# Attention and SoLU on one core: aligned arrays, centring on ScalarE, clamps on GpSimd, and a new list of steps

## The chip, the core and the metric

The kernel runs on one core of a Trainium2 chip. The metric is the device time of one execution in microseconds. The engines are named as in the profile: PE is TensorE, PEld its weight loads, DVE is VectorE, ACT is ScalarE, POOL is GpSimd, SP the engine that issues most DMAs. Each engine takes its own instructions strictly in the order of its list and waits at an instruction whose inputs or buffers aren't ready.

## The reference

Windowed attention (8 batches, 8 heads, 576 positions, 64 wide), then a SoLU block over all 4608 tokens. Half of the heads attend to the last 32 positions, half to every fourth of the last 128.

```python
scores = scale * np.matmul(q, k.transpose(0, 1, 3, 2))
scores = np.where(masks[None, :, :, :], scores, -1000000000.0)
attn = softmax(scores) @ v                      # per head
x = attn.transpose(0, 2, 1, 3).reshape(B * S, H * D)   # 4608 x 512
h = x @ w_in                                    # 4608 x 1024
e = np.exp(h - h_max)
solu = h * e / (np.sum(e, axis=-1, keepdims=True) + 1e-09)
mu = np.mean(solu, axis=-1, keepdims=True)
var = np.mean((solu - mu) ** 2, axis=-1, keepdims=True)
ln = (solu - mu) / np.sqrt(var + 1e-06) * g_ln
out = ln @ w_out                                # 4608 x 512
```

The softmax is abridged here. The weights w_in and w_out arrive as 64-bit floats, whose words the kernel turns into 32-bit floats itself.

## The kernel before, in words

**Units and tiles.** Attention is cut into 32 units (two heads of one batch each), taken one at a time for units 0 to 3 (steps S, max, sub, exp, sum, inv, norm, turn, V, x) and two at a time from there (the same names with a p in front, pS2 for units 4 and 5). The tokens are 36 tiles of 128, in 18 pairs; four units, one batch, give the 576 tokens of four and a half tiles.

**Weights.** Each of 16 blocks of 128x512 64-bit words (0 to 7 of w_in, 8 to 15 of w_out) is loaded (w) and converted: abs and low on ACT pick the upper and lower words, clamp (L261) bounds the magnitude, sign (L267) and join (L274) on DVE put the bits together, gain multiplies w_out's rows by g. Every float is then split into a high and a low half (hi, lo), since products run with 32-bit operands rounded for PE and each product takes three matmuls: high by high, high by low, low by high. The low half is either a difference on PE copied by ACT (diff and lo, LOW_DIFF "m") or a subtraction on POOL ("p").

**Products.** Tiles 0 to 3, the first two pairs, are computed plainly: ha, hb, hc, hd are quarters of x @ w_in (6 matmuls of 512 columns each; 24 a tile). All later pairs use seven products Ma to Mg of sums instead of eight. For these, eight sums of weight blocks are made once (ta to td, each for j = 0 and 1, L316), with their own high and low halves (ua to ud on ACT, va to vd by the subtraction of L296), and sums of x for every pair (s on DVE, hS and lS its halves).

**SoLU.** For a tile: peak (the maximum, L533, where h is in PSUM), e (the exponential, L537), gate (L543: h times e, its sum in mu), mid (L551 scales mu, L557 subtracts the mean), var (a square on ACT, L562, and six one-column instructions on POOL), t (8 transposes on PE, L577), th and tl (halves of the transposed tile, L584 and L296), o (24 matmuls with w_o, L606), out (L613 scales by 1/sigma, and a DMA).

**Buffers.** Everything has a fixed address in SBUF. t and e are two buffers each, th and tl two each, ob one; qt, kt and vt are four each, so that unit 4's v is loaded into unit 0's buffer. The conversions borrow them: mag (the magnitudes) lies in slots of the weight sums and in ob, low in x_sum and in slot w12, and the 64-bit words in t, e, th and tl. All arrays begin at multiples of 64 bytes; the identity matrices, the mask and minus begin 128 above a multiple of 512, w_i, w_o, x, t, e, sm, pt, qt, kt and vt 384 above one, and the slots w8 to w13, th and tl 192 above.

**Order.** No scheduler moves anything. ORDER is one long list of steps, written out in the source; the program walks it once, and each step appends its instructions to the lists of its engines. A step early in ORDER thus stands early on every engine that it uses, including the two DMA queues. The loads of one SP list follow each other too: one that waits for its buffer holds up those behind it.

Of the kernel before, what the change touches and what calls it, by code (L numbers as in the profile page):

```python
# [38 lines left out]
POOL_NORM = ()  # L39
ACT_MID = ()  # L40
# [3 lines left out]
LOW_DIFF = "mmmmmmpppppppppp"  # L44
# [74 lines left out]
def windowed_attention_then_solu_kernel(  # L119
# [26 lines left out]

    id_sb = fixed("id_sb", [P])
    minus = fixed("minus", [P], F32R)
    id_bf = fixed("id_bf", [2 * P], BF16)[:, 0:P]
    mask_sb = fixed("mask_sb", [2, NS * WQ], BF16)  # L150
# [14 lines left out]
    g_sb = fixed("g_sb", [FT])  # L165
    mx_sb = fixed("mx", [2, 2, NS])
    rs_sb = fixed("rs", [2, 2, NS])
    pk_sb = fixed("pk", [2, 2])
    mhalf = fixed("mhalf", [1])
    below = fixed("below", [1])  # L170
# [89 lines left out]
    def conv_clamp(b):  # L260
        nc.vector.tensor_scalar(  # L261
            out=mag(b), in0=mag(b), scalar1=F64_MIN, scalar2=F64_MAX, op0=ALU.max, op1=ALU.min
        )
# [43 lines left out]
    def w_sum(k, j):  # L307
        b11, b12, b21, b22 = (mag(b) for b in (2 * j, 2 * j + 1, 4 + 2 * j, 5 + 2 * j))
        out, a, b = {
            "a": (b11, b12, b11),  # L310
            "b": (x_spare[:, 512 * j : 512 * j + 512], b22, b12),
            "c": (b22, b22, b11),
            "d": (b21, b21, b22),
        }[k]
        sums[k, j] = out
        nc.gpsimd.tensor_tensor(out=out, in0=a, in1=b, op=ALU.subtract)  # L316
# [7 lines left out]
    def w_sum_lo(k, j):  # L324
        w = w_sum_slot(k, j)
        rest(nc.gpsimd, w[:, 1, :], sums[k, j], w[:, 0, :])
# [328 lines left out]
    for name in PRODUCTS:  # L655
        do[name] = quick(name)
# [80 lines left out]
```

## Time and profile before

| | |
|---|---|
| median of 3 runs | 562.0 us (561.88 to 562.92) |
| the profiled execution's own time | 561.86 us |
| its span, first to last instruction | 560.1 us |
| mean granted TensorE clock | 0.963 |
| instructions | 16524 |

The page gives the busy time of each engine over the span and then the same in 40 slices of 14 us, in tenths:

```profile
PE   1747678999989999998999999989999999999997
...
DVE  4997999686886668775879767876896966648350
ACT  5658567454634446452554453533644545335350
POOL 0103797844324134150425242331524433021130
PEclk9958959999999999997999999998999999999999
```

In the first seven slices the weights are converted and the first attention units run; behind them PE is the busiest engine. PEclk is the granted TensorE clock, in tenths. A row such as "L606 PE MATMUL banks<-w_o,th" names the line of the program, the engine, the operation, what is written and what is read. In the chain of waits a row is a start, a duration and the engine and line whose end released the next row.

### The profile page before, as it was taken

The page shows a single profiled execution, that of the slowest core. Times are in us where ns is not written, and L with a number is a line of the kernel's source. Part 1 is how long each engine was busy: PE and PEld are TensorE (multiplying, and loading weights), DVE is VectorE, ACT ScalarE, POOL GpSimd, SP SyncE. Part 2 cuts the span into 40 slices and gives each one's busy share as a digit, 9 for nine tenths or more (in the row PEclk, how much of TensorE's full clock was granted, in tenths as well). Part 3 has the DMA queues.
Part 4 walks back from the last instruction along what each step waited for, and adds up shares of the span by engine and source line. Part 5 has one row for each costly group of instructions (what it writes and reads, how often), then busy time and mean ns, then how long its engine had stood idle before and what let it go on. Part 6 is the DMA issues. An engine that isn't in the chain of part 4 may idle for free.

```text
span 560.1 us, 16524 instructions
## 1 busy us (share of the span) xinstructions
PE 504.6 (90%) x7322; PEld 407.3 (73%) x7322; DVE 411.2 (73%) x692; ACT 273.0 (49%) x430; POOL 192.0 (34%) x274
## 2 busy tenths in 40 slices
PE   1747678999989999998999999989999999999997
PEld 0445566787878788886888788777777788888875
DVE  4997999686886668775879767876896966648350
ACT  5658567454634446452554453533644545335350
POOL 0103797844324134150425242331524433021130
PEclk9958959999999999997999999998999999999999
DMA  8967240315113323003052111533222000000001
GB/s 274 372 236 249 93 149 2 94 48 188 73 55 103 98 72 110 22 19 122 20 184 76 64 52 64 167 110 104 73 86 78 20 21 19 20 19 36 23 34 42
DMA packets 22247, 51.66 MB, mean 92 GB/s; under 512 B 2720, under 2 KB 3360, under 8 KB 22176
## 3 DMA queue, kind: packets, MB, share of 16 engines
q1 hardware_dynamic: 22032, 50.48, 26.9%
q8 instruction: 57, 0.93, 0.7%
q10 hardware_dynamic: 144, 0.13, 0.1%
q14 instruction: 14, 0.11, 0.1%
HBM read 41.16 MB, written 9.44 MB: 90 GB/s over the span
## 4 chain that ended last, share of the span: by engine, by line
PE 80%; DVE 9%; DMA 5%; issue 3%; ACT 1%; SPq 1%; ACTq 0%; DVEq 0%
PE banks L606 34%; PE banks L480 29%; PE banks L433 6%; PE banks L577 6%; PE banks L348 5%; DMA vt<-vw 2%; DVE t L557 2%; DMA kt<-kT 1%; DMA t<-w_in 1%; DVE x_sum L267 1%; DVE sm L374 1%; DVE t L543 1%; DVE mx L387 1%; DVE nmax L533 1%; ACT x_raw L449 1%
## 5 line engine op out<-in xcount | busy, mean ns | idle before, releaser
L606 PE MATMUL banks<-w_o,th 128*128 128x512 f32 x576 | 183.0, 401 | 1.2 <-issue 0.8
L606 PEld LDWEIGHTS banks<-w_o,th 128*128 128x128 f32 x576 | 107.5, 189 | 27.1 <-ACT ob L613 1.0
L606 PE MATMUL banks<-w_o,tl 128*128 128x512 f32 x288 | 113.2, 397 | 0.1
L480 PE MATMUL banks<-w_i,x_hi 128*128 128x512 f32 x320 | 104.8, 408 | 1.3 <-issue 1.3
L391 POOL TENSOR_TENSOR sm<-sm,mx 128x1280 f32<-128x1280 f32 x14 | 39.7, 2839 | 131.2 <-DVE mx L387 92.6
L480 PEld LDWEIGHTS banks<-w_i,x_hi 128*128 128x128 f32 x320 | 59.6, 193 | 14.1 <-issue 1.7
L480 PE MATMUL banks<-w_i,x_lo 128*128 128x512 f32 x160 | 64.0, 400 | 2.0 <-DVE sm L374 1.2
L606 PEld LDWEIGHTS banks<-w_o,tl 128*128 128x128 f32 x288 | 54.5, 189 | 14.5 <-issue 1.5
L480 PE MATMUL banks<-w,x_hi 128*128 128x512 f32 x192 | 61.6, 402 | 0.0
L537 ACT ACTIVATE e<-t,nmax 128x1024 f32<-128x1024 f32 x32 | 36.7, 1148 | 49.9 <-DVE nmax L520 49.9
L514 DVE CUSTOM_DVE_ANT_0 t<-banks,t 128x512 f32<-128x512 f32 x64 | 43.3, 686 | 22.8 <-PE banks L480 21.8
L613 ACT ACTIVATE ob<-banks,rstd 128x512 f32<-128x512 f32 x36 | 24.9, 693 | 65.6 <-PE banks L606 46.7
L433 PE MATMUL banks<-pt,vt 32*64 32x64 f32 (+3 forms) x2816 | 37.1, 242 | 20.9 <-issue 8.1
L507 DVE TENSOR_TENSOR t<-banks,t 128x512 f32<-128x512 f32 x32 | 22.1, 690 | 45.7 <-PE banks L480 28.3
L433 PEld LDWEIGHTS banks<-pt,vt 32*64 32x64 f32 x2816 | 34.7, 144 | 27.1 <-issue 11.4
L296 DVE TENSOR_TENSOR tl<-banks,th 128x512 fp32r<-128x512 f32 x72 | 45.9, 678 | 11.3 <-ACT th L584 11.2
L584 ACT CAST th<-banks 128x512 fp32r<-128x512 f32 x72 | 38.9, 594 | 21.2 <-PE banks L606 11.4
L412 POOL TENSOR_TENSOR sm<-sm,rs 128x1280 f32<-128x1280 f32 x14 | 34.0, 2429 | 37.6 <-DVE rs L407 31.9
L562 ACT ACTIVATE e<-t 128x1024 f32<-128x1024 f32 x36 | 38.1, 1059 | 17.6 <-DVE t L557 17.5
L543 DVE CUSTOM_DVE_ANT_0 t<-t,e 128x1024 f32<-128x1024 f32 x32 | 38.9, 1219 | 8.3 <-ACT e L537 8.3
L348 PE MATMUL banks<-kt,qt 64*32 64x64 f32 x2560 | 33.3, 235 | 12.2 <-issue 8.8
L348 PEld LDWEIGHTS banks<-kt,qt 64*32 64x32 f32 x2560 | 28.9, 110 | 20.1 <-issue 14.9
(94 smaller groups left out, 780.3 us busy)
## 6 DMA issues: line engine op xcount, KB each, us to landing
vt<-vw SPq DMA_DIRECT2D x32, 384.0 KB, 4.8
kt<-kT SPq DMA_DIRECT2D x32, 312.0 KB, 4.1
qt<-qT SPq DMA_DIRECT2D x32, 296.0 KB, 4.6
out<-ob SPq DMA_DIRECT2D x35, 256.0 KB, 2.0
e<-w_in SPq DMA_DIRECT2D x2, 512.0 KB, 5.5
t<-w_in SPq DMA_DIRECT2D x2, 512.0 KB, 7.4
t<-w_out SPq DMA_DIRECT2D x2, 512.0 KB, 6.8
e<-w_out SPq DMA_DIRECT2D x2, 512.0 KB, 6.4
```

The costliest lines, as they stand in the source:

```text
L296: eng.tensor_tensor(out=out, in0=whole, in1=part.bitcast(F32), op=ALU.subtract)
L348: nc.tensor.matmul(out=ps[WIN * c : WIN * c + WIN, h, WQ * i : WQ * i + WQ], lhsT=qt[D * h : D * h + D, q0 : q0 + WIN], rhs=kt[D * h : D * ...
L391: eng.tensor_tensor(out=rows(part(sm_sb, us)), in0=soft_source(us), in1=wide(part(mx_sb, us)), op=ALU.subtract,)
L412: eng.tensor_tensor(out=sm, in0=sm, in1=wide(part(rs_sb, us)), op=ALU.mult)
L433: nc.tensor.matmul(out=ps[D * h : D * h + D, c, c0 : c0 + k1 - k0], lhsT=vt[WIN * c : WIN * c + WIN, i, D * h : D * h + D], rhs=pt[WIN * c ...
L480: nc.tensor.matmul(out=ps, lhsT=x[:, xs + k], rhs=weights(ws[k])[:, part, :], start=start and k == 0 and j == 0, stop=stop and k == 1 and ...
L514: nc.vector.tensor_tensor_reduce(out=split_t(k)[half], in0=banks[:, c, :], in1=add, scale=1.0, scalar=-3.0e38, op0=ALU.add, op1=ALU.max, a ...
L537: nc.scalar.activation(out=e_sb[i % 2], in_=h_of(i), func=AF.Exp, bias=ms[i]["nmax"], scale=1.0, accum_out=se)
L543: nc.vector.tensor_tensor_reduce(out=t_sb[i % 2], in0=h_of(i), in1=e_sb[i % 2], scale=1.0, scalar=0.0, op0=ALU.mult, op1=ALU.add, accum_ou ...
L562: nc.scalar.activation(out=e_sb[i % 2], in_=t_sb[i % 2], func=AF.Square, accum_out=sq)
L584: nc.scalar.copy(out=turned("th", i)[:, 4 * c : 4 * c + 4], in_=ps_t(i, c))
L606: nc.tensor.matmul(out=ps_o(i), lhsT=a[:, f, :], rhs=w_o[:, f, part, :], start=k == 0, stop=k == 3 * FT - 1,)
```

## The change

Six things differ.

1. The small arrays (g, the attention's maxima and sums, pk and two constants) become parts of one array, `little`, of 384 bytes, and the mask is padded, so that id, minus, mask, w_i, w_o, all parts of x, t, e, ob, sm, pt, qt, kt, vt, the slots w8 to w13, th and tl begin at multiples of 512 bytes.
2. The centring of every tile (mid) runs on ACT as an activation with a bias; DVE only scales mu by −1/1024 for it.
3. The 16 clamps run on POOL.
4. The eight sums of weight blocks and their eight low halves run on DVE, not POOL; the norms of units 0 to 3 run on POOL, not DVE.
5. Blocks 6 and 7 get their low halves by a difference on PE and a copy on ACT.
6. ORDER is a new list, and in it an output product o (24 matmuls) is four steps oa, ob, oc, od of six, with other steps allowed in between.

```diff
-LOW_DIFF = "mmmmmmpppppppppp"
+LOW_DIFF = "mmmmmmmmpppppppp"
...
+    little = fixed("little", [96])
+    g_sb, mhalf, below = little[:, 0:FT], little[:, 8:9], little[:, 9:10]
+    mx_sb = little[:, 16:36].rearrange("p (u h s) -> p u h s", u=2, h=2)
...
-    mask_sb = fixed("mask_sb", [2, NS * WQ], BF16)
+    mask_sb = fixed("mask_sb", [768], BF16)[:, 0 : 2 * NS * WQ]
...
     def conv_clamp(b):
-        nc.vector.tensor_scalar(
+        nc.gpsimd.tensor_scalar(
             out=mag(b), in0=mag(b), scalar1=F64_MIN, scalar2=F64_MAX, op0=ALU.max, op1=ALU.min
         )
...
         sums[k, j] = out
-        nc.gpsimd.tensor_tensor(out=out, in0=a, in1=b, op=ALU.subtract)
+        nc.vector.tensor_tensor(out=out, in0=a, in1=b, op=ALU.subtract)
...
-        rest(nc.gpsimd, w[:, 1, :], sums[k, j], w[:, 0, :])
+        rest(nc.vector, w[:, 1, :], sums[k, j], w[:, 0, :])
...
-        eng = nc.gpsimd if len(us) == 2 or us[0] in POOL_NORM else nc.vector
-        eng.tensor_tensor(out=sm, in0=sm, in1=wide(part(rs_sb, us)), op=ALU.mult)
+        nc.gpsimd.tensor_tensor(out=sm, in0=sm, in1=wide(part(rs_sb, us)), op=ALU.mult)
...
     def moe_centre(i):
...
+        nc.vector.tensor_scalar(out=mu, in0=mu, scalar1=-1.0 / DF, scalar2=None, op0=ALU.mult)
+        nc.scalar.activation(out=t, in_=t, func=AF.Identity, bias=mu, scale=1.0)
...
-    def moe_o(i, lo=0, hi=3 * FT):
+    def moe_o(i, lo, hi):
...
+    for k, name in enumerate(("oa", "ob", "oc", "od")):
+        do[name] = lambda i, k=k: moe_o(i, 6 * k, 6 * k + 6)
```

What stands beside the steps named here in the two lists, ORDER around pturn3, the transpose of units 6 and 7's probabilities (pV3 is their product with v, t, o and the M products are as above):

```
before: ... peak2 gain15 th0 tl0 hb3 var1 pturn3 hd3 peak3 e2 hi15 q9 gate2 gain14 hi14 pV3 ud0 lo14 e3 gate3
        lo15 mid3 px3 hA2 lo13 o0 ud1 mid2 hB2 lA2 Ma2 vd0 v8 vd1 pS4 ...
after:  ... pnorm3 lo14 hb3 mid2 var2 ua0 tl1 peak3 pturn3 e3 oa0 td0 ob0 oc0 pV3 tc1 va1 td1 ub0 vb0 ud0 od0
        va0 ud1 vd1 vd0 px3 hA2 q8 pS4 ...
```

On PE around pV3, the product of the attention's units 6 and 7 (L433, with vt_93 and vt_94), before (L480 is the last quarter of a plain tile, L606 the first output product):

```order
L480 MATMUL banks<-w_i,x_lo 128x512
L433 MATMUL banks<-pt,vt_93 64x64 x24
L433 MATMUL banks<-pt,vt_93 64x48 x8
L433 MATMUL banks<-pt,vt_93 64x16 x8
L433 MATMUL banks<-pt,vt_94 64x64 x24
L433 MATMUL banks<-pt,vt_94 64x48 x8
L433 MATMUL banks<-pt,vt_94 64x16 x8
L606 MATMUL banks<-w_o,th_1109 128x512 x2
L606 MATMUL banks<-w_o,tl_1112 128x512
```

And at the same place in the changed kernel (L603 is L606 of before, L436 is L433, and vt_94 and vt_95 are units 6 and 7):

```order
L603 MATMUL banks<-w_o,th_1084 128x512 x2
L603 MATMUL banks<-w_o,tl_1087 128x512
L436 MATMUL banks<-pt,vt_94 64x64 x24
L436 MATMUL banks<-pt,vt_94 64x48 x8
L436 MATMUL banks<-pt,vt_94 64x16 x8
L436 MATMUL banks<-pt,vt_95 64x64 x24
L436 MATMUL banks<-pt,vt_95 64x48 x8
L436 MATMUL banks<-pt,vt_95 64x16 x8
L603 MATMUL banks<-w_o,th_1084 128x512 x2
```

Eighteen of the first output product's matmuls now stand ahead of pV3, and six behind it.

On DVE around the first gate and the transpose of units 4 and 5 (pturn2, the STREAM_TRANSPOSE), before; t_76, e_78 and mu belong to tile 0:

```order
L543 ISA t_76,mu<-banks,e_78 128x1024
L543 ISA mu 128x1
L551 TENSOR_SCALAR mu<-mu 128x1
L557 TENSOR_SCALAR t_76<-t_76,mu 128x1024
L261 TENSOR_SCALAR w_290<-w_290 128x512
L267 SCALAR_TENSOR_TENSOR w_107<-tl_756,w_107 128x512
L415 STREAM_TRANSPOSE pt<-sm 128x1280
```

In the changed kernel (t_77 and e_79 are tile 0's there, L546 is L543, L553 is L551, L418 is L415):

```order
L546 ISA t_77,mu<-banks,e_79 128x1024
L546 ISA mu 128x1
L536 TENSOR_REDUCE nmax<-banks 128x1
L553 TENSOR_SCALAR mu<-mu 128x1
L271 SCALAR_TENSOR_TENSOR w_122<-e_80,w_122 128x512
L418 STREAM_TRANSPOSE pt<-sm 128x1280
```

The centring and the clamp are gone from DVE, and tile 1's peak (L536) stands between the gate and mu's scaling. POOL's list begins, behind its constants, with the clamps and the single units' norms:

```order
L265 TENSOR_SCALAR w_100<-w_100 128x512
L265 TENSOR_SCALAR w_111<-w_111 128x512
L265 TENSOR_SCALAR w_100<-w_100 128x512
L265 TENSOR_SCALAR w_111<-w_111 128x512
L415 TENSOR_TENSOR sm<-sm,little 128x640 x2
L265 TENSOR_SCALAR w_243<-w_243 128x512
L265 TENSOR_SCALAR w_303<-w_303 128x512 x2
```

Before, its first array instructions were two sums of weights (L316); all clamps (L265 here) and these norms (L415 here) were DVE's.

More of the change, by code (lines that the diff above doesn't have):

```diff
@@ L38 @@
 PE_MASK = (0, 1, 2, 3)
-POOL_NORM = ()
-ACT_MID = ()
 REBIAS = 2.0**16
@@ L145, in fixed @@
         return const.tile([P, *shape], dtype, name=name)
+    little = fixed("little", [96])
+    g_sb, mhalf, below = little[:, 0:FT], little[:, 8:9], little[:, 9:10]
+    mx_sb = little[:, 16:36].rearrange("p (u h s) -> p u h s", u=2, h=2)
+    rs_sb = little[:, 40:60].rearrange("p (u h s) -> p u h s", u=2, h=2)
+    pk_sb = little[:, 64:68].rearrange("p (k c) -> p k c", k=2)
     id_sb = fixed("id_sb", [P])
@@ L149, in windowed_attention_then_solu_kernel @@
     id_bf = fixed("id_bf", [2 * P], BF16)[:, 0:P]
-    mask_sb = fixed("mask_sb", [2, NS * WQ], BF16)
+    mask_sb = fixed("mask_sb", [768], BF16)[:, 0 : 2 * NS * WQ]
+    mask_sb = mask_sb.rearrange("p (d w) -> p d w", d=2)
     w_i = fixed("w_i", [8, 2, 512], F32R)
@@ L164, in windowed_attention_then_solu_kernel @@
     vts = [fixed(f"vt{k}", [NV, 2 * D]) for k in range(4)]
[L165 to L170, printed above, removed]
     banks = psum.tile([P, 8, 512], F32, name="banks")
@@ L549, in moe_centre @@
         t, mu = t_sb[i % 2], ms[i]["mu"]
-        on_act = i in ACT_MID
-        nc.vector.tensor_scalar(
-            out=mu, in0=mu, scalar1=(-1.0 if on_act else 1.0) / DF, scalar2=None, op0=ALU.mult
-        )
-        if on_act:
-            nc.scalar.activation(out=t, in_=t, func=AF.Identity, bias=mu, scale=1.0)
-        else:
-            nc.vector.tensor_scalar(out=t, in0=t, scalar1=mu, scalar2=None, op0=ALU.subtract)
+        nc.vector.tensor_scalar(out=mu, in0=mu, scalar1=-1.0 / DF, scalar2=None, op0=ALU.mult)
+        nc.scalar.activation(out=t, in_=t, func=AF.Identity, bias=mu, scale=1.0)
     def moe_var(i):
@@ L651, in windowed_attention_then_solu_kernel @@
         "peak": moe_peak, "e": moe_exp, "gate": moe_gate, "mid": moe_centre, "var": moe_var,
-        "t": moe_t, "th": moe_th, "tl": moe_tl, "o": moe_o, "out": moe_out,
-        "oa": lambda i: moe_o(i, 0, 21), "oz": lambda i: moe_o(i, 21),
-    }
+        "t": moe_t, "th": moe_th, "tl": moe_tl, "out": moe_out,
+    }
+    for k, name in enumerate(("oa", "ob", "oc", "od")):
+        do[name] = lambda i, k=k: moe_o(i, 6 * k, 6 * k + 6)
     for name in PRODUCTS:
```

126 rows, old and new, of the table ORDER are left out of this document.

## The prediction

> **What bounds the kernel now.** I begin with the page's busy shares, its PE slices (14 us each) and its chain that ended last, and then read the table of windows by stage. In the slices all digits below 8 that are not the last lie in the first seven, up to 98 us.
>
> ```profile
> PE 504.6 (90%) x7322; PEld 407.3 (73%) x7322; DVE 411.2 (73%) x692; ACT 273.0 (49%) x430; POOL 192.0 (34%) x274
> ...
> PE   1747678999989999998999999989999999999997
> ...
> PE 80%; DVE 9%; DMA 5%; issue 3%; ACT 1%; SPq 1%; ACTq 0%; DVEq 0%
> ```
>
> ```profile
> 0.00:100.00 100.00, 61.88 (x1496) 47.23 (x1497) 85.08 (x120) 64.98 (x103) 44.29 (x41) 0.85 0.57 193
> 20.00:100.00 80.00, 55.23 (x1274) 43.19 (x1275) 73.23 (x99) 54.69 (x88) 44.10 (x37) 0.81 0.48 168
> 40.00:94.50 54.50, 39.94 (x718) 31.29 (x717) 49.61 (x59) 36.15 (x59) 36.47 (x27) 0.81 0.38 126
> 100.00:550.00 450.00, 436.46 (x5803) 355.35 (x5802) 326.08 (x573) 206.62 (x325) 147.67 (x234) 0.99 0.22 71
> ```
>
> The first figure behind a window's length is PE's busy time, the third DVE's, the fifth POOL's. Up to 100 us PE works 61.9 us and idles 38.1. From 100 to 550 it works 436.5 of 450, so at most 13.5 us can be won there by any rearrangement. Two stages, then. From 20 to 100 us DVE is busy 73.2 of 80 and the opening is DVE's; behind that PE is the limit and DVE has a quarter of its time free. PE's waits up to 100 us say what it waits for:
>
> ```profile
> PE banks L340 <- DMA id_bf<-ident_bf: 10.3, 1, 10.3
> PE banks L433 <- DVE pt L415: 6.7, 2, 5.5
> PE banks L433 <- DMA vt<-vw: 6.0, 3, 3.7
> ```
>
> The 10.3 us at the start stay; 12.7 us are waits for the attention's transposes on DVE and for v by DMA. From the chain in order of time (start, us):
>
> ```profile
> 93.04 1.43 DVE pt L415
> ...
> 96.78 5.94 PE banks L606 x24
> ...
> 114.43 5.55 PE banks L480 x24
> 119.98 5.60 PE banks L606 x24
> ```
>
> The opening ends with the transpose for the attention's second pair (pturn3, to 94.47); from 96.78 PE hardly stops. I follow DVE to the end of pturn3, and PE from there to Mb2, the first product with a weight sum (114.43).
>
> **The change part by part.** Durations over the whole run:
>
> ```profile
> L557 DVE TENSOR_SCALAR t<-t,mu x36: 752/754/2931, 64.1 to 537.7; 128x1024 f32<-128x1024 f32 x36
> L261 DVE TENSOR_SCALAR w<-w x13: 384/420/1502, 5.9 to 85.3; 128x512 f32<-128x512 f32 x13
> L412 DVE TENSOR_TENSOR sm<-sm,rs 128x640 f32<-128x640 f32 x4 | 3.3, 823 | 0.1
> L412 POOL TENSOR_TENSOR sm<-sm,rs 128x1280 f32<-128x1280 f32 x14 | 34.0, 2429 | 37.6 <-DVE rs L407 31.9 <-DVE mu L551 5.8
> L543 DVE CUSTOM_DVE_ANT_0 t<-banks,e 128x1024 f32<-128x1024 f32 x4 | 4.8, 1203 | 0.1
> L533 DVE TENSOR_REDUCE nmax<-banks 128x1 f32<-128x1024 f32 x4 | 4.8, 1204 | 0.0
> L537 ACT ACTIVATE e<-t,nmax 128x1024 f32<-128x1024 f32 x32 | 36.7, 1148 | 49.9 <-DVE nmax L520 49.9
> ```
>
> DVE's work up to pturn3, at undisturbed durations. Gone: 16 clamps at the median 0.42, 6.7 us; four norms of 0.82, 3.3; the centrings of tiles 0 and 1 at 0.75, 1.5. New: in the new order five of the eight sums stand ahead of pturn3, at 0.68 (the 512-wide L267 beside an idle POOL, below), 3.4; and gate2 and peak3, which stood behind pturn3, stand in front of it, 1.2 each (L543, L533). Net 11.5 − 5.8, **−5.7 us**.
>
> DVE's stalls beside POOL. The same groups in the window from 40 to 94.5 us, POOL's and DVE's:
>
> ```profile
> L316 POOL TENSOR_TENSOR w<-w,w 128x512 f32<-128x512 f32 x4 | 6.0, 1491 | 0.2
> L296 POOL TENSOR_TENSOR w_i<-w,w_i 128x512 fp32r<-128x512 f32 x4 | 5.4, 1346 | 25.2 <-ACT w_i L285 25.2
> L316 POOL TENSOR_TENSOR x_sum<-w,w 128x512 f32<-128x512 f32 x2 | 3.4, 1697 | 1.8 <-DVE w L274 1.8
> L296 POOL TENSOR_TENSOR w<-x_sum,w 128x512 fp32r<-128x512 f32 x1 | 1.3, 1279 | 0.0
> ...
> L267 DVE SCALAR_TENSOR_TENSOR x_sum<-th,x_sum 128x512 int32<-128x512 int32 x2 | 4.6, 2310 | 0.0
> L557 DVE TENSOR_SCALAR t<-t,mu 128x1024 f32<-128x1024 f32 x2 | 3.4, 1703 | 0.1
> ```
>
> L557 takes 1.70 here against 0.75, and L267's two take 2.31 each; in the window up to 40 us, where POOL is nearly idle, two of the same kind took:
>
> ```profile
> L267 DVE SCALAR_TENSOR_TENSOR x_sum<-th,x_sum 128x512 int32<-128x512 int32 x2 | 1.4, 680 | 0.0
> ```
>
> Such excesses (2.31 − 0.68) over all of DVE's instructions of this window come to some 10 us, an estimate from the same view. POOL's work there is 36.5 us by the windows. The four rows, 16.1 us, leave it: sums and their low halves for DVE, two lows of w_in for PE and ACT. Some eight clamps arrive. A clamp on POOL is in no row: between nothing and POOL's dearest 512-wide row, 1.7, I take 0.8, half the row of two inputs, since it reads one array: 6.4 us. That leaves 26.8 on POOL, and stalls in proportion, 10 × 26.8/36.5 = 7.3: **−2.7 us**. Bounds: −10 with no stall left; −0.7 with clamps at 1.7, and +3 if the five sums are then stalled to twice their length on DVE too.
>
> [...]
>
> What DVE waits for anew. The norms of units 0 to 3 take half of 2.43 on POOL, 1.2 instead of 0.82, with a crossing there and back before each transpose; each of 16 joins follows a clamp on POOL; gate0 stands in front of pturn2 and waits for ACT's exponential, and joins and pturn2 queue behind it. Of these 20 hand-overs most have other DVE work listed in between. I take 0.2 each, **+4 us**, the bounds being 0 and the 8.4 that DVE wins above.
>
> So pturn3 ends at 94.5 − 5.7 − 2.7 + 4 ≈ 90.1. On SP's list, before, the load of v4 stood ahead of v2; it writes v0's buffer and was issued when V0 had ended, and v2 behind it landed at 37.15:
>
> ```profile
> 31.71 0.33 SPq L182
> ...
> 32.08 5.07 DMA vt<-vw
> ```
>
> Now v2 and v3 go out ahead of v4 and v5, but behind w12, which writes a buffer that sign4 on DVE has to have read, and all later loads queue behind it. The clamps and norms that leave DVE there, and joins put later, take some 4 us off the first four transposes; v2 has to come that much earlier too, and has room for it as v4 no longer stands in its way. POOL takes norm0 and norm1 behind clamp3, so w3 must have landed for them; it is issued ahead of units 2 and 3. The two further weight differences on PE (four 512-wide matmuls) lie in its idle 38 us.
>
> From pturn3 to Mb2. Before, 114.43 − 94.47 = 20 us: pV3, o0, Ma2, pS4, o1, t3, t2. Now oa0, ob0 and oc0 stand in front of pV3, where PE waits for pturn3: three quarters of 5.60, −4.2. On DVE eleven sums and low halves, 7.5 us at 0.68, are new here and the second pair's centrings go; Mb2's sums of x and its weight sum may be late, for which I take +1 (bounds 0 and 6). Mb2 starts at 90.1 + 20 − 4.2 + 1 ≈ 106.9, **7.5 us earlier**.
>
> Behind Mb2. Products, transposes and outputs are the same. An output product in four words of six matmuls lets others in between and fills the same bank. ACT gains 36 centrings at about 1.15 (L537, which has a bias too), 41 us on 273, and from gate to transposes the way is some 0.55 longer than with 0.75 on DVE and a crossing; the activation behind it (L562), which followed DVE, now follows its own engine. PE has other products listed between a gate and its t, so I cost this at nothing; without that cover it is 0.55 × 32 = 18 us. The tail has the same steps.
>
> Alignment. Every large array now begins at a multiple of 512 bytes; before, w_i and x began 384 above one, w_o too, th and tl 192 above. 24 matmuls took 5.60 in L606 (w_o with th, unlike residues) and 5.55 in L480, 233 and 231 ns each. In the opening, plain products with w_i and x (like residues) stand 9 periods of three apart between these rows of PE's timeline:
>
> ```profile
> 52.38 0.63 PE L480 MATMUL banks<-w_i,x_hi 128*128 128x512 f32 x2
> ...
> 58.52 0.62 PE L480 MATMUL banks<-w_i,x_hi 128*128 128x512 f32 x2
> ```
>
> That is 6.14/27 = 227 ns. If like residues were the cause, the 864 output matmuls and the 672 of products with sums would go to 227: −8. If nothing depends on it, 0. I take **−2.8**, the output matmuls falling 3 ns, half way, and keep −8 and, since a common start could also collide, +3 as ends.
>
> [...]
>
> **Sum.** 560.1 − 7.5 − 2.8 = 549.8 of span. Before, the execution took 561.86, 1.76 beyond its span and 0.1 under the median of 562.0; with 1.76 again, **551.6 us**.
>
> **The rivals.**
> A, alignment decides: all matmuls at 227 or less, −8 to −14, with the opening's −7.5: 540 to 546, and lower with more. For it, the spread from 227 to 233; against it, that the 227 stand in a window whose granted clock is 0.81, with much else different.
> B, the opening's gain is eaten: DVE's hand-overs cost the 8.4 that its work and stalls save, Mb2's inputs come 5 late in place of 1, and alignment gives nothing. Mb2 then starts at 94.5 + 20 − 4.2 + 5 = 115.3, 0.9 later than before, 562.8 in all, and up to 5 less where one of these holds in part: 558 to 563. For it, 16 joins and four transposes behind POOL; against it, 5.7 us of plain DVE work gone.
> C, slower: centring in ACT's list waits behind casts and exponentials of up to 1.1 and delays each tile's transposes by the 0.55 and more. It decides where PE's listed work between gate and t is shorter than that way, which takes about 1.2 for gate, 1.15 for centring and the queue on ACT, some 3 to 5 us. On 32 tiles uncovered that is 18 against 10 won: 563 to 572. Against it, PE idles only 13.5 us in 450 now, so that such covers exist in every pair; for it, a wholly new order in which no row shows them.
>
> **How the numbers follow.** Forecast (opening −3 to −14, alignment −6 to +1) 0.58, A 0.12, B 0.15, C 0.15. The range, 537 to 563, takes in the forecast, A's main part and B. A measurement of this kernel can tell some 0.2% (1.1 us) from no change: B splits into 0.09 faster, 0.05 same and 0.01 slower, and C is slower: faster 0.79, same 0.05, slower 0.16.
>
> **What would show it.** The transpose ahead of pV3 ends near 90; oa0 to oc0 lie ahead of pV3; Mb2 starts near 107; L267 stays near 0.68 in the opening; POOL's clamps take near 0.8; behind 100 us PE is busy 436 of 450 again; 24 output matmuls in a row take 5.53. The steps are wrong if DVE idles for POOL's clamps or norms, if PE's transposes wait for ACT's centring, or if the output matmuls keep their 5.60 or fall far below it.

## The result, and the profile after

| | before | changed |
|---|---|---|
| median of 4 runs | 561.98 us (561.88 to 562.92) | 540.95 us (539.1 to 542.35) |
| the profiled execution's own time | 561.86 us | 539.1 us |
| its span | 560.1 us | 537.2 us |
| start of Mb2 on PE | 114.19 us | 108.68 us |

The changed kernel is faster: ratio 0.962, with an interval of 0.959 to 0.965. The forecast had the sign, and 551.6 in place of 541: it saw half of the gain. One execution below is left out for a slower state, the profiled one of the kernel with the sums on POOL (555.1 us), from which an expectation still took 7.7 us. From the page of the changed kernel, the busy shares and the slices of PE (13.4 us each):

```profile
PE 496.1 (92%) x7328; PEld 406.0 (76%) x7328; DVE 370.6 (69%) x652; ACT 311.7 (58%) x468; POOL 201.8 (38%) x276
...
PE   1849688999999999998999899989999899999997
```

PE does the same matmuls and six 512-wide pieces more, yet is busy 8.5 us less: matmuls have become shorter. The windows of the changed kernel (PE, PEld, DVE, ACT, POOL, then the granted clock):

```profile
0.00:100.00 100.00, 70.00 (x1673) 52.25 (x1673) 77.12 (x112) 72.03 (x115) 67.54 (x57) 0.86 0.54 193
40.00:91.00 51.00, 43.09 (x653) 32.62 (x651) 43.30 (x56) 40.64 (x67) 38.43 (x31) 0.89 0.40 142
100.00:527.00 427.00, 419.69 (x5629) 348.76 (x5630) 293.47 (x541) 238.33 (x352) 134.24 (x219) 1.00 0.22 75
```

In the first 100 us DVE is busy 8 us less and POOL 23 more, and PE gets 8.1 us more work in. Behind that PE idles 7.3 us in 427, where it idled 13.5 in 450. PE's waits behind 100 us, first of the kernel before, then of the changed one (total, times, longest):

```profile
PE banks L348 <- issue: 5.3, 5, 1.7
PE banks L433 <- issue: 4.9, 3, 2.7
PE banks L480 <- issue: 1.3, 1, 1.3
PE banks L577 <- DVE t L557: 1.0, 2, 0.7
PE banks L606 <- issue: 0.8, 1, 0.8
```

```profile
PE banks L436 <- issue: 6.7, 4, 1.8
PE banks L352 <- issue: 0.3, 1, 0.3
PE banks L603 <- issue: 0.2, 1, 0.2
```

Nearly all of it is "issue": PE waits for no semaphore. Ten such waits of 12.3 us have become six of 7.2.

To split the 22.9 us of span I took the ends of all consecutive PE instructions of both traces: how far apart 512-wide matmuls end (where under 300 ns), how much they are beyond that where they end some 427 ns apart, and every other stop of more than 240 ns, all behind the start of Mb2. Ends 427 ns apart are called half speed here: the granted clock is 0.50 or 0.51 there, from 259.2 to 266.0 and from 378.7 to 382.1 us before, and from 361.6 to 365.0 in the changed kernel.

| part | before | changed | difference |
|---|---|---|---|
| up to the start of Mb2 | 114.2 us | 108.7 us | −5.5 |
| spacing of 816 output matmuls | 233.3 ns | 227.8 ns | −4.5 |
| spacing of some 666 product matmuls | 231.3 ns | 227.8 ns | −2.3 |
| stops of PE | 17.1 us | 9.2 us | −7.9 |
| matmuls at half speed | 3.9 us | 1.4 us | −2.5 |

The parts sum to −22.7. The forecast had −7.5 for the first line, −2.8 for the next two, and nothing for the last two.

### The profile page after: what moved, and what is told of

It is laid out like the page before. It is cut to its first block, busy times and chain, and to the rows that moved or that the text cites. A ratio compares the mean times of both kernels' runs of the same rounds, so it can differ in the third digit from the quotient of the medians.

```text
span 537.2 us, 16553 instructions
## 1 busy us (share of the span) xinstructions
PE 496.1 (92%) x7328; PEld 406.0 (76%) x7328; DVE 370.6 (69%) x652; ACT 311.7 (58%) x468; POOL 201.8 (38%) x276
## 4 chain that ended last, share of the span: by engine, by line
PE 84%; DVE 4%; POOL 3%; issue 3%; ACT 3%; DMA 2%; SPq 0%; DVEq 0%; POOLq 0%; ACTq 0%
PE banks L603 37%; PE banks L483 31%; PE banks L436 6%; PE banks L574 6%; PE banks L352 5%; POOL w L265 2%; DMA t<-w_in 1%; DMA vt<-vw 1%; DVE little L406 1%; DVE w L278 1%; POOL sm L415 1%; ACT w_i L289 1%; ACT w L254 0%; DVE x_sum L271 0%; DVE pt L418 0%
## 5 line engine op out<-in xcount | busy, mean ns | idle before, releaser
L603 PE MATMUL banks<-w_o,th 128*128 128x512 f32 x576 | 180.6, 397 | 0.1
L603 PEld LDWEIGHTS banks<-w_o,th 128*128 128x128 f32 x576 | 106.1, 188 | 22.3 <-ACT ob L610 0.6
L603 PE MATMUL banks<-w_o,tl 128*128 128x512 f32 x288 | 111.9, 393 | 0.2 <-issue 0.2
L395 POOL TENSOR_TENSOR sm<-sm,little 128x1280 f32<-128x1280 f32 x14 | 40.7, 2909 | 139.6 <-DVE little L391 139.6
L603 PEld LDWEIGHTS banks<-w_o,tl 128*128 128x128 f32 x288 | 54.4, 189 | 12.3 <-issue 0.6
L436 PE MATMUL banks<-pt,vt 32*64 32x64 f32 (+3 forms) x2816 | 36.5, 236 | 20.7 <-issue 11.8
L436 PEld LDWEIGHTS banks<-pt,vt 32*64 32x64 f32 x2816 | 33.8, 137 | 27.6 <-issue 15.8
L546 DVE CUSTOM_DVE_ANT_0 t<-t,e 128x1024 f32<-128x1024 f32 x32 | 42.9, 1342 | 11.3 <-ACT e L540 11.3
L452 ACT COPY x_raw<-banks 128x1152 f32<-128x1152 f32 (+1 forms) x18 | 27.0, 1517 | 36.1 <-PE banks L436 36.1
L554 ACT ACTIVATE t<-t,mu 128x1024 f32<-128x1024 f32 x36 | 41.2, 1149 | 10.2 <-DVE mu L553 10.2
L415 POOL TENSOR_TENSOR sm<-sm,little 128x1280 f32<-128x1280 f32 (+1 forms) x18 | 37.7, 2097 | 23.6 <-DVE little L411 22.7
L560 POOL TENSOR_SCALAR se<-se 128x1 f32<-128x1 f32 x36 | 17.8, 494 | 67.7 <-ACT e L540 65.4
L483 PEld LDWEIGHTS banks<-w,x_hi 128*128 128x128 f32 x192 | 35.8, 191 | 7.2
```

The lines of the kernel that those rows point to most:

```text
L395: eng.tensor_tensor(out=rows(part(sm_sb, us)), in0=soft_source(us), in1=wide(part(mx_sb, us)), op=ALU.subtract,)
L415: nc.gpsimd.tensor_tensor(out=sm, in0=sm, in1=wide(part(rs_sb, us)), op=ALU.mult)
L436: nc.tensor.matmul(out=ps[D * h : D * h + D, c, c0 : c0 + k1 - k0], lhsT=vt[WIN * c : WIN * c + WIN, i, D * h : D * h + D], rhs=pt[WIN * c ...
L483: nc.tensor.matmul(out=ps, lhsT=x[:, xs + k], rhs=weights(ws[k])[:, part, :], start=start and k == 0 and j == 0, stop=stop and k == 1 and ...
L546: nc.vector.tensor_tensor_reduce(out=t_sb[i % 2], in0=h_of(i), in1=e_sb[i % 2], scale=1.0, scalar=0.0, op0=ALU.mult, op1=ALU.add, accum_ou ...
L554: nc.scalar.activation(out=t, in_=t, func=AF.Identity, bias=mu, scale=1.0)
```

## The experiments

Each kernel is compared with the kernel before on the same chip; ratios are to be held against the changed kernel's 0.962 (0.959 to 0.965). Chips differ: the kernel before had medians of 562 to 564 us on those used here.

### The addresses

The first undoes the new addresses in the changed kernel, the second makes them alone in the kernel before.

```diff
# addresses undone, from the changed kernel
-    little = fixed("little", [96])
-    mask_sb = fixed("mask_sb", [768], BF16)[:, 0 : 2 * NS * WQ]
+    mask_sb = fixed("mask_sb", [2, NS * WQ], BF16)
...
+    g_sb = fixed("g_sb", [FT])
+    mx_sb = fixed("mx", [2, 2, NS])
```

> The changed kernel with the arrays' old addresses; all else as changed. Theory 1 (the addresses set the spacing of 512-wide matmuls): spacing back from 228 to 231-233 ns on some 1,530 matmuls, so about 7 us slower than the changed kernel (541 to 548), with the opening and PE's pauses unchanged. Rival (the spacing fell because other engines now use SBUF differently): spacing stays 228, time 541.

> The kernel before with the new addresses alone. Theory 1: spacing 228 in place of 231-233, 562 becomes 555 (-7), PE's pauses and the opening as before. Rival (other engines' traffic): 562, spacing 233. If the addresses act through DMA or DVE too, the opening's end (Mb2 at 114.4) moves as well.

Undone: 550.9 us, ratio 0.978 (0.973 to 0.982); spacing 233.2 and 231.3 ns, the old values to 0.1. Alone: 557.6 us, 0.989 (0.984 to 0.994); spacing 227.5 and 228.0. Rows of the chains that ended last, one of each kernel, tell the same: 18 output matmuls, and two times 24.

```profile
228.56 4.20 PE banks L603 x18
```

```profile
238.45 5.44 PE banks L606 x24
...
247.52 5.44 PE banks L606 x24
```

4.20 for 18 is 233 ns with the old addresses, 5.44 for 24 is 227 with the new ones, where the kernel before had 5.60. The opening's end hardly moved (Mb2 at 110.0 in the first, 114.8 in the second). The addresses set the spacing, whichever list and engines the kernel has.

Which addresses? Two kernels add bytes: 128 ahead of all arrays, and 384 behind w_i and w_o.

```diff
# all arrays 128 up
-    little = fixed("little", [96])
+    little = fixed("little", [128])
# all but w_i and w_o 384 up
+    fixed("gap", [96])
     x_raw = fixed("x_raw", [KT, RING])
```

> The changed kernel with 128 bytes more ahead of all arrays: every large array begins 128 above a multiple of 512. If a like distance of both operands is what counts: spacing 228, ratio 0.962. If the multiple of 512 itself counts: spacing 231 or more, some 5 to 8 us slower, ratio 0.972 to 0.977.

> The changed kernel with 384 bytes more behind w_i and w_o: these, the moving operands of all output matmuls, stay at multiples of 512, and all others, the stationary operands x, th and tl among them and the weight sums in slots w8 to w13, move 384 up. If the moving operand sets the spacing: output matmuls 228, products in between (part of their moving operands are the slots). If the stationary one does: 231 to 233 for both. If only a difference between the two counts: output matmuls 233, products near 231.

All at 128: 542.9 us, 0.963 (0.958 to 0.968), spacing 227.7 and 227.6. All but the weights at 384: 550.3 us, 0.977 (0.973 to 0.981), spacing 232.7 and 231.8. So it isn't the multiple of 512. The same with 384 and 192:

> The changed kernel with all large arrays 384 above a multiple of 512. If a like distance of both operands is all that counts: 228 ns, as with 0 and 128. If the distance itself counts too (matmuls of w_i with x, both at 384, took 229 to 231 in the kernel before): 230 ns, some 3 us slower.

> The changed kernel with all large arrays 192 above a multiple of 512, no multiple of 128. Like distance alone: 228. If it has to be a multiple of 128 as well: 230 to 233.

542.8 us, 0.964 (0.953 to 0.975), and 541.7, 0.962 (0.954 to 0.971), with 227.8 and 227.6, and twice 227.8 ns. Four common distances, one spacing. What counts is that the arrays lie alike, and the change's multiple of 512 is one of the four tried. It isn't settled which pairs must: in the kernel with all but the weights at 384, products of the slots w8 to w13 with x, both at 384, took 229 to 231 ns with w_i and w_o at 0, not 227.

### PE's stops

From PE's timeline of the changed kernel, with the wait ahead of a row in brackets:

```profile
243.76 1.46 PE L436 MATMUL banks<-pt,vt 32*64 32x64 f32 x117
246.88 0.40 PE L436 MATMUL banks<-pt,vt 32*64 32x48 f32 x18 [1.65 <-issue]
...
360.88 0.41 PE L436 MATMUL banks<-pt,vt 32*64 32x48 f32 x21 [1.85 <-issue]
361.22 0.89 PE L483 MATMUL banks<-w_i,x_hi 128*128 128x512 f32 x2
361.91 0.63 PE L483 MATMUL banks<-w_i,x_lo 128*128 128x512 f32 x1
```

A run of small attention matmuls stops in its middle for no semaphore. Counting weight loads, matmuls and waits for semaphores in PE's list, the four long stops behind 100 us come at instructions 7616, 9408, 11200 and 12992, all 192 above a multiple of 256, and in both kernels no other stop of this kind comes elsewhere. Each follows 256 instructions that PE ran through in 1.6 us; where such a stretch behind 96 us took over 3.5 us, 76 times in the two kernels, there were two stops of more than 0.24 us, of 0.8 and 0.3. The page's third part, on DMA queues, has a queue for instructions, with 57 transfers of 16 KB each:

```profile
q8 instruction: 57, 0.93, 0.7%
```

PE's list has some 14,700 instructions, 57 times 256 being 14,592. The four stops' distances, 1,792 or seven times 256 each, fit transfers of 256 instructions.

The trace also has the start of each of these transfers. Ahead of the four long stops of the changed kernel the last one began at 244.45, 299.33, 358.28 and 418.71 us, and PE went on at 246.88, 301.77, 360.88 and 421.06, 2.3 to 2.6 us later each time; ahead of the eight stops of over 0.7 us behind 100 us in the kernel before it was 2.3 to 2.4 us. They also count alike: 29 transfers had begun before PE went on at instruction 7616, which is 29 × 256 + 192, and 50 at 12,992, which is 50 × 256 + 192. By these counts PE waits at these stops for its next 256 instructions, which is inferred: the trace names no releaser there. A short stretch alone doesn't make a stop: in the kernel with 48 instructions more, below, one that ran in 1.6 us ended at 435.7 us without any, and there the transfer had begun 4.2 us ahead. What makes a transfer start earlier or later is not shown.

The stops then depend on where borders every 256 instructions fall, and can be moved without moving any work. Tiny matmuls on zeros, written to a bank not yet in use, go in front of PE's list while PE has nothing to do.

```diff
+    for _ in range(24):                       # 128 in the control
+        nc.tensor.matmul(
+            out=banks[0:32, 7, 0:8], lhsT=blank.bitcast(BF16)[:, 0:32],
+            rhs=blank.bitcast(BF16)[:, 32:40], start=True, stop=True, skip_group_check=True,
+        )
     for step in ORDER.split():
```

> The changed kernel with 24 tiny matmuls (48 PE instructions) more at PE's start, in its idle time there; nothing else moves. Theory 2 (PE pauses wherever a stretch of 256 of its instructions, counted from a fixed position, runs in less than some 3.3 us, and the new list happens to put the borders well): the borders now fall so that 14 stretches behind 96 us are that short where 7 were, about 11 us slower, 541 to 552. Rival (the pauses went since output products are cut into four and lie between attention matmuls, wherever the borders are): within 2 us of 541.

> Control for the one before: 128 tiny matmuls (256 PE instructions), which shift the borders by exactly one stretch. Theory 2: the same borders, 541 within 1 us, pauses at the same places as in the changed kernel. If the tiny matmuls themselves cost, it is slower by the opening's delay only. Rival to both (any shift costs): as slow as with 48.

With 48 instructions: 554.0 us, 0.984 (0.979 to 0.988), 12 us more than the changed kernel; Mb2 at 108.0, spacing 227.7 twice, stops 21.2 us, half-speed matmuls 5.5. PE's longest waits behind 96 us, of this kernel and of the control:

```profile
PE banks L354 <- issue: 7.4, 6, 2.3
PE banks L438 <- issue: 6.9, 5, 2.3
PE banks L605 <- issue: 2.2, 1, 2.2
PE banks L354 <- ACT x_raw L454: 1.7, 1, 1.7
```

```profile
PE banks L438 <- issue: 7.7, 4, 2.4
PE banks L605 <- issue: 0.2, 1, 0.2
```

In the control, with 256 instructions, the four long stops come at 247, 306, 367 and 426 us, in the same places of the same four attention pairs as in the changed kernel at 247, 302, 361 and 421; with 48 they come elsewhere, in scores (L354) too. (Its wait for ACT lies ahead of Mb2, at 98 us.) The control took 546.6 us, 0.970 (0.965 to 0.975), some 4 us more than the changed kernel, where at most 1 was expected: its stops were longer (10.8 us, and 4.5 at half speed), the four long ones in the same places. Its queue for instructions has one transfer more, for 256 more instructions on PE and one elsewhere:

```profile
q8 instruction: 58, 0.95, 0.8%
```

The length of a stop varies, from 1.5 to 2.4 us among the four of the control.

The list before, too, moved by 82 instructions:

> The kernel before with 41 tiny matmuls (82 PE instructions) more at PE's start. Theory 2 holds for the old list too: 14 stretches of 256 instructions behind 96 us then run in less than 3.3 us where 9 do now, and the shortfall below 3.3 us grows by 8 us: 8 us slower or somewhat more, ratio 1.012 to 1.02. Rival (the old list's pauses come from elsewhere): ratio 1.000.

575.3 us, 1.020 (1.013 to 1.028), with Mb2 at 114.6, stops 24.1 us for 17.1 and 9.4 us at half speed for 3.9: 12.5 more, where 8 or somewhat more was expected, the half-speed part having been left out of it.

The last one removes stops: at six places one product of six matmuls is moved from beside a pair of attention products to the middle of it, so that no 256 instructions there take less than 3 us. Nothing is added.

```diff
-"cd7 ce7 pV8 px8 lA8 cc7 Mg7 cg7"
+"cd7 ce7 V16 Mg7 V17 px8 lA8 cc7 cg7"
-"oc25 od25 out25 pV14 hB14"
+"oc25 V28 od25 out25 V29 hB14"
...
```

> The changed kernel with six of its attention pairs' products with v (V, units 4 and 5, 6 and 7, 16 and 17, 20 and 21, 24 and 25, 28 and 29) cut in two, with one six-matmul product that stood next to them put in between, so that no stretch of 256 PE instructions there runs in less than 3 us. Theory 2: the four pauses of some 2 us behind Mb2, and the half-speed matmuls behind the longest of them, go: 8 to 11 us less, and 1 to 2 in the opening; ratio to before 0.943 to 0.949, about 531. Rival (the pauses come from attention matmuls as such): they stay in the cut pieces, ratio 0.96.

534.3 us (532.7 to 535.3), 0.949 (0.945 to 0.952): faster than both. PE's longest waits behind 96 us:

```profile
PE banks L481 <- DVE t L508: 1.3, 1, 1.3
PE banks L350 <- issue: 1.2, 2, 0.8
PE banks L481 <- DVE little L515: 0.4, 1, 0.4
```

The long stops are gone, none of the matmuls behind Mb2 ran at half speed, and 1.3 us of a wait for DVE came in their place, where Mg7 now stands closer behind what it needs. Not all of the gain lies there: Mb2 started at 106.2 us, 2.5 earlier than in the changed kernel, so that some 4 of the 6.6 us that its span is shorter lie behind Mb2, where 8 to 11 were expected.

### Which engine does what

Three of the four moves are undone alone in the changed kernel, and all four together. (The norms of units 0 to 3 weren't undone alone, nor were the low halves of blocks 6 and 7 by a difference on PE.)

```diff
# centring on DVE
-        nc.scalar.activation(out=t, in_=t, func=AF.Identity, bias=mu, scale=1.0)
+        nc.vector.tensor_scalar(out=t, in0=t, scalar1=mu, scalar2=None, op0=ALU.subtract)
# clamps on DVE
-        nc.gpsimd.tensor_scalar(
+        nc.vector.tensor_scalar(
# sums and their low halves on POOL
-        nc.vector.tensor_tensor(out=out, in0=a, in1=b, op=ALU.subtract)
+        nc.gpsimd.tensor_tensor(out=out, in0=a, in1=b, op=ALU.subtract)
```

> The changed kernel with the centring of all tiles back on DVE. My theory (both engines have slack behind the opening, so where the centring runs doesn't show there): PE's pauses and spacing as in the changed kernel, the opening's end 1 to 2 us later since tiles 0 to 3's centrings return to DVE; ratio to before 0.962 to 0.966. Rival (the centring off DVE is a source of the gain behind the opening, through shorter waits for the transposes): ratio 0.975 or more, with PE waiting for L557's kind ahead of its transposes.

> The changed kernel with the 16 clamps back on DVE. My step priced the clamps at 6.7 us of DVE up to pturn3, partly given back as waits for POOL. Theory 3 (the waits for POOL's clamps, at 1.9 us each rather than the 0.8 that I took, ate most of that): the opening's end moves by less than 2 us either way, ratio 0.960 to 0.967. Rival (the clamps on POOL carry the opening's gain): Mb2 4 us later or more, ratio 0.970.

> The changed kernel with the eight weight sums and their low halves back on POOL. If DVE beside POOL is what bounds the opening, 11 us less on DVE and 22 more on POOL there: PE may get Mb2's weights later, by up to 5 us, or earlier if DVE's queue was the limit. Theory: within 3 us of the changed kernel, ratio 0.957 to 0.968. Pauses and spacing unchanged.

> The changed kernel's list and addresses with all four engine moves undone (centring, clamps, single norms on DVE, sums on POOL). If their parts add up as measured alone (Mb2 3 us later without centring on ACT, 3.6 without clamps on POOL, 7.7 without sums on DVE): Mb2 14 us later, near 123, ratio 0.985 to 0.99. Theory (clamps and sums trade places between the same two engines, so undoing both hurts less than the sum): Mb2 near 117, ratio 0.975 to 0.98. Pauses and spacing as in the changed kernel.

| undone | us | ratio (interval) | start of Mb2, us |
|---|---|---|---|
| none (changed kernel) | 540.95 | 0.962 (0.959 to 0.965) | 108.7 |
| centring | 547.1 | 0.972 (0.968 to 0.976) | 111.7 |
| clamps | 543.8 | 0.967 (0.962 to 0.971) | 112.3 |
| sums | 548.6 | 0.973 (0.968 to 0.978) | - |
| all four | 555.4 | 0.986 (0.982 to 0.990) | 119.4 |

The centring and the sums are worth time in the new list, each clear of the intervals; of what all four are worth, some 13 us, 10.7 arise up to Mb2. Centring: my theory had 1 to 2 us of opening and got 3; the rival's waits for L554 (L557 of before) ahead of transposes came to 0.6 us in one place. Its ratio is higher than 3 us account for; its stops were longer too (12.9 us for 9.2), and what part of that is the centring's stays open. Clamps: Mb2 3.6 us later, between the theory's 2 and the rival's 4; at the end 2.5 us are left of it, and the intervals overlap, so that a gain of the clamps alone isn't shown. All four: 10.7 us later at Mb2, between the two numbers expected, and spacing and places of the stops as in the changed kernel. The waits of PE up to 118 us in that kernel say where from:

```profile
PE banks L437 <- DVE pt L419: 13.0, 4, 6.7
...
PE banks L484 <- DVE mu L547: 5.8, 1, 5.8
```

against these in the changed one, up to 100 us, behind the wait for the mask, which both have:

```profile
PE banks L436 <- DMA vt<-vw: 6.0, 2, 5.2
PE banks L483 <- DVE mu L546: 5.1, 1, 5.1
PE banks L436 <- issue: 5.0, 3, 2.1
PE banks L436 <- DVE pt L418: 1.7, 2, 1.1
```

It is the transposes of probabilities on DVE that come late, 13.0 us for 1.7, as the prediction's way through DVE had it. Part of that stands in place of the 6.0 us for v, for which the changed kernel waits at these products and the other doesn't.

The other half: the new engines and addresses in the old list.

```diff
-POOL_NORM = ()
-ACT_MID = ()
+POOL_NORM = (0, 1, 2, 3)
+ACT_MID = tuple(range(36))
# and clamps on POOL, sums on DVE, the new addresses
```

> The kernel before with all the new engine assignments (centring on ACT, clamps on POOL, sums on DVE, single norms on POOL) and the new addresses, in the old list of steps with o in one piece. Theory: spacing 228 (-7), PE's pauses as before (some 17 to 20 us behind Mb2, since PE's list is the old one); what is left against the addresses alone (ratio 0.989) is the engines' part. If the engine moves carry the opening's 5.6 us: ratio 0.979. Rival (it is the list that carries it; the old list wasn't made for these engines): 0.989 or slower.

579.1 us, 1.028 (1.023 to 1.033): slower than before, and 21 us slower than the addresses alone. Mb2 starts at 122.9, 8 us later than with the addresses alone. PE's longest waits behind 110 us:

```profile
PE banks L606 <- ACT ob L613: 5.8, 2, 4.2
PE banks L433 <- issue: 4.8, 4, 2.3
PE banks L348 <- issue: 3.6, 4, 1.7
PE banks L577 <- ACT t L555: 3.5, 3, 1.8
```

Transposes wait for the centring on ACT (L555), and output products for ob behind it on ACT: the kind of wait of rival C, in the list that wasn't made for it. With 3.5 and 5.8 us these waits are a part of the 21; the opening's 8 is another.

## Why the prediction was half right

**The opening: right in its way, 2 us too much.** It followed DVE to the end of pturn3 and PE from there. Of the changed kernel's chain:

```profile
89.52 1.52 DVE pt L418
91.05 0.04 issue
91.09 1.75 PE banks L436 x108
92.84 2.09 issue
```

pturn3 ended at 91.0 (90.1 forecast, 94.5 before), and from there Mb2 took 17.6 us (16.8 forecast). 2.1 of these are a stop in pV3 at a border of 256, which I hadn't looked for; the six output matmuls behind it took 2.69 us where six take 1.36 further on. Mb2 came 5.5 us earlier, not 7.5. One price was far off: the clamp on POOL, 0.8 by the number of arrays it reads.

```profile
L265 POOL TENSOR_SCALAR w<-w 128x512 f32<-128x512 f32 x13 | 26.6, 2061 | 12.9 <-ACT w L254 12.7
```

2.06 us, above the dearest 512-wide row that I took for the upper end (1.7). At that price POOL was busy 38.4 us from 40 to 91 us, more than before, and not the 27 forecast. Yet the stalls on DVE did not grow with it. In the same window of the changed kernel:

```profile
L271 DVE SCALAR_TENSOR_TENSOR x_sum<-th,x_sum 128x512 int32<-128x512 int32 x2 | 2.8, 1414 | 0.1
L278 DVE SCALAR_TENSOR_TENSOR w<-w,w 128x512 int32<-128x512 int32 x4 | 4.7, 1182 | 2.7 <-POOL w L265 2.5
...
L278 DVE SCALAR_TENSOR_TENSOR w<-w,x_sum 128x512 int32<-128x512 int32 x2 | 1.4, 686 | 0.8 <-POOL w L265 0.8
```

L271 took 1.41 where L267 took 2.31 before; four joins (L278) took 1.18, two others 0.69, and their waits for POOL's clamps are 3.3 us. Over all of DVE's instructions of the two windows, what goes beyond the short durations of the same kinds fell from some 12 us to some 5, an estimate from the traces, where the forecast had 2.7 less. So stalls don't go in proportion to POOL's busy time. Their cause isn't shown: no run here tells which of POOL's instructions held up which of DVE's. That pturn3 ended within 1 us of its forecast is thus in part luck: the clamp was priced too low and the relief from stalls too low as well.

**Spacing: right cause, wrong size.** The step read 227 ns in matmuls with operands that lie alike, 231 to 233 in others, and then took half of the output matmuls' difference, 2.8 us, as "half way". The runs show all of it, for both kinds: 6.8 us, within 1.2 of the 8 that the step gave as its end. Hedging between two ends that the trace had told apart cost 4 us. With all arrays alike the mean was 227.5 to 228.4 in every kernel; the +3 for starts that collide rested on no row, and no run shows it.

**Behind Mb2: the step that failed.** "Products, transposes and outputs are the same. An output product in four words of six matmuls lets others in between and fills the same bank." No term for PE's stops came from that, though the waits behind 100 us were 12.3 us of issue, and the page's 13.5 us of idle time were named as what could be won at most. No reason stands there for leaving them out. They belong to stretches of 256 instructions, and the new list puts far fewer short ones on borders: 10.4 us with the half-speed matmuls that follow some of the stops. Those matmuls count as busy (3.4 of the 3.4 us from 361.6 in the changed kernel), so that the 13.5 was no upper limit either. That it was the list's borders and not the cutting of o as such is what the kernel with 48 tiny matmuls shows: o stays cut there, and the 12 us are gone.

**Rivals.** A (alignment decides, 540 to 546) has the measured time in its range, but not the mechanism: alignment gave 6.8, not 8 to 14. The 14 is in no run: it would have taken some 223 ns, an estimate from 9 ns on each of 1,536 matmuls, and the lowest mean of any kernel was 227.5. B did not happen. C's waits for the centring on ACT showed only under the old list, a few long ones and not one for every tile; that the 21 us there are near the 18 of its price is chance.

## What to carry to other kernels

- When PE waits for "issue" again and again, count instructions between the waits. If they lie whole multiples of one number apart, here of 256, mix long matmuls into runs of short ones, so that no such stretch runs through in under 3 us; six matmuls in each of six places were worth over 1%.
- Give all arrays that meet in matmuls, and those around them, the same distance from a multiple of 512 bytes. It costs some padding and gave 1.5 to 2.4% of a matmul's time here.
- Work moved to another engine is worth what the order of the list lets it be: the same four moves gained about 13 us in the list made for them and lost 21 in the old one.

## What the runs showed of the hardware that was not expected

- The mean spacing of 512-wide matmuls was 227.5 to 228.4 ns in every kernel whose arrays all lay alike (0, 128, 192 or 384 above a multiple of 512), and 231 to 233 in every one with mixed distances, with any division of work between the other engines.
- By the counts above, 57 transfers of 16 KB for some 14,700 instructions, PE's list came 256 instructions at a time, and where PE ran through 256 short ones in 1.6 us it mostly stopped, until 2.2 to 2.9 us after the next transfer had begun, in the two kernels and those with shifted borders.
- Behind some stops the next matmuls ran at half speed. From the timeline of the kernel before, and then the window of these matmuls, with the granted clock third from the end:

```profile
259.83 0.41 PE L433 MATMUL banks<-pt,vt 32*64 32x16 f32 x8 [2.67 <-issue]
260.17 1.22 PE L480 MATMUL banks<-w_i,x_hi 128*128 128x512 f32 x2
261.19 0.63 PE L480 MATMUL banks<-w_i,x_lo 128*128 128x512 f32 x1
```

```profile
259.20:266.00 6.80, 6.17 (x22) 4.88 (x23) 1.75 (x5) 2.07 (x2) 0.00 (x0) 0.50 0.37 118
```

  Their ends lie 427 ns apart in place of 231, for 13 matmuls, 2.5 us beside the stop's own 2.7. The length of a stop alone doesn't decide it: 1.85 us at 361 us in the changed kernel was followed by it, 1.88 in the control was not; in the kernel with 48, 1.76 at 259 us was and 2.21 at 233 us was not.
- A two-operation TENSOR_SCALAR on 128x512 took 2.06 us on POOL (mean of 13, changed kernel) and 0.42 on DVE (median of 13, kernel before), though it reads one array; POOL's sums of two such arrays took 1.49 and 1.70 in the kernel before.
